# Two chain flows in the written order of a recurrent attention, and z rows kept in the u tile

## The chip, the core and the metric

The kernel runs on one core of one Trainium2 chip. The metric is device time of one execution in microseconds, the median of three runs. The kernel before takes 2223.99 us (2222.03 to 2224.59). A core has TensorE (PE in the profile) for matrix products into PSUM, VectorE (DVE), ScalarE (ACT) and GpSimd (POOL) for elementwise work, and SyncE (SP), whose queue issues all DMAs of this kernel. Each engine works through its own queue in the order in which the program wrote it, and waits at an instruction until what that needs is there.

## The reference

Three parts follow each other. First a recurrent attention: 4 batches x 8 heads, 768 tokens, head dimension 40, with a 40 x 40 state for each head.

```
for t in range(S):
    y[:, :, t] = einsum('bhd,bhde->bhe', r_t, state)
    Sa = einsum('bhde,bhe->bhd', state, a_t)
    state = state * w_t - outer(Sa, b_t) + outer(v_t, k_t)
```

Then a mixture of 8 experts over 3072 tokens of width 320 (hidden width 1024), where every expert computes every token and a gate matrix P, balanced by 8 rounds of row and column scaling, weighs them. Last a network that takes the maximum of three products (width 768) and multiplies it by an output matrix. All is fp32.

## The kernel before

**Blocks and units.** The recurrence over tokens is turned into matrix products over blocks of C = 128 tokens. There are NJ = 6 blocks j and 4 batches b, so 24 units n = 4j + b, each with 8 heads. Batches don't depend on each other; a unit depends on the same batch of the block before through its state. The work of a unit has four parts, written as Python generators:

- `scales` (function `decays`, lines 300 to 339): running products of w on VectorE, `bt` and `at`, and `off` on ScalarE (line 338), a range check. `off` and the result tile `yt` share one buffer.
- `labs` (`lab_grams`): products of `bt` and `at`, copied to `lab` and `ld` by ScalarE. After four units `ld` is turned to `lt`; `invert` inverts its 32 x 32 triangles on GpSimd (block 0 mostly on VectorE), and the result `tt` is turned to `td` on VectorE (line 379).
- `pre`: masked products `lak` (matmul at line 348, mask at line 420), then z (line 475 is its last part). Its first matmuls, tp at line 439, may run once the post of unit n-2 and the chain of unit n-2 are complete (`count["post"] >= n - 1 and count["chain"] >= n - 1`).
- `chain`: a triangular solve in four rows of 32 tokens. For row i: subtract the effect of earlier rows (line 499, i > 0), copy z to `zs` (ScalarE, line 503), multiply by the inverted triangle `td` (line 507), copy the result to `u` (line 511). Each step needs the one before. The chain of unit n may start when pre of unit n is written, post of unit n-2 is complete and `td` of the block exists.
- `post`: turns `u` (ups, line 523), adds up y (lines 534 and 546), updates the state (lines 561 to 569), multiplies and stores y (lines 576 and 579).

**The order.** All parts run in one program order that a planner in the kernel's Python writes while the program is built. Each part yields a `Seg`: an estimated time on TensorE (`pe`), an engine that follows (`eng`, `cost`), what it needs, and a gate on the counts of finished parts. `drive` (line 723) holds one `Flow` for each kind of part and always takes one segment: first a segment without TensorE work that can start now; else the first TensorE segment that can start, in the order of the list of flows (where a running measure of TensorE's load is low, the one with the most load, except that the flow `first`, the chains, goes ahead); else the earliest, with spare matmuls (`idle`, line 708) written into the gap. Beside these flows runs `fill`: parts of the first expert for blocks that are already done, from unit 4 on. The planner's times are its own estimates; they are not measured.

**After the attention.** From about 640 us on `networks` runs the rest of the experts and the last network, with matmuls at lines 215 and 223.

The chains are one flow before the change: `Flow(counted("chain", (chain(n) for n in range(units))))`. `zs` has a single buffer; `u` has two, by n % 2.

Of the kernel before, what the change touches and what calls it, by code (L numbers as in the profile page):

```python
# [9 lines left out]
F32 = mybir.dt.float32  # L10
F32R = mybir.dt.float32r
I32 = mybir.dt.int32
AF = mybir.ActivationFunctionType
# [4 lines left out]
NB, H, S, D = 4, 8, 768, 40  # L18
C = 128
# [14 lines left out]
WARM = 0.55  # L34
# [8 lines left out]
FALL = 0.4  # L43
LATE = 17
SLACK = 0.8
AHEAD = 4
TICK = 10.24 / 3
LAG = 0.2
WLO, WHI = 0.8, 1.25
# [3 lines left out]
def hx(h):  # L53
    return 4 * (h % 2) + h // 2
# [16 lines left out]
def tile_kernel(ctx, tc, em, tm, qr, qk, qv, qw, qa, qb, w_gate, w1, w2, u1, u2, u3, u_out, out):  # L71
    nc = tc.nc

    def pool(stack, name, bufs=1, **kw):
        return stack.enter_context(tc.tile_pool(name=name, bufs=bufs, **kw))
# [170 lines left out]
    ws, xf, first, gate = [{} for _ in pieces], [], [], []  # L246
    order = [NJ - 2, NJ - 1] + list(range(NJ - 2))


    units = NB * NJ  # L250
    with ExitStack() as st:
# [8 lines left out]
        chp = pool(st, "ch")  # L260
# [8 lines left out]
        def jb(n):  # L269
            return n // NB, n % NB  # L270
# [209 lines left out]
        def chain(n):  # L480
            j, b = jb(n)
            d, u = un[n], u_ring[n % 2]
            s = None
            for i in range(4):
                r = slice(32 * i, 32 * i + 32)
                if i == 0:
                    s = Seg(
                        eng="A", cost=0.32, needs=lambda: [d["z_"], blk[j]["t_"]],
                        gate=lambda: count["pre"] > n and count["post"] >= n - 1 and "t" in blk[j],
                    )  # L490
                    yield s
                    zh = d["z"].rearrange("t g a x -> t (g a) x")
                    lab, td = d["lab"], blk[j]["t"]
                    zs = chp.tile([C, H, D], F32, tag="zs", name="zs")
                else:
                    s = Seg(pe=0.23, w=0.3, eng="A", cost=0.32, needs=[s])
                    yield s
                    for h in range(H):
                        nc.tensor.matmul(  # L499
                            zh[r, h, 0:D], lhsT=lab[0:32 * i, hx(h), 32 * i - 32:32 * i], rhs=u[0:32 * i, h, 0:D],  # L500
                            start=False, stop=True, skip_group_check=True, tile_position=(0, 32 * i),
                        )
                nc.scalar.activation(out=zs[r], in_=zh[r, :, 0:D], func=AF.Copy)  # L503
                s = Seg(pe=0.24 if i else 0.62, w=0.25, eng="A", cost=0.32, needs=[s])
                yield s
                for h in range(H):
                    nc.tensor.matmul(  # L507
                        zh[r, h, 0:D], lhsT=td[r, 8 * b + hx(h), :], rhs=zs[r, h, :],
                        start=(h == 0), stop=True, skip_group_check=True, tile_position=(32 * i, 32 * i),
                    )  # L510
                nc.scalar.activation(out=u[r, :, 0:D], in_=zh[r, :, 0:D], func=AF.Copy)
            d["u_"] = s
# [137 lines left out]
        clk = dict(E=2.0, V=2.0, A=3.5, P=6.0, D=1.0, warm=False, acc=0.0, h=0.0)  # L650
        RATE = dict(V=(0.3, 2.1e-3), P=(0.4, 4.5e-3))

        def spend(t, w, floor=False):

            left = t - clk["E"] if floor else t
            while left > 1e-6:
                pace = 1.0 if floor or clk["warm"] else 0.5
                tick = TICK - clk["E"] % TICK
                d = min(left / pace, tick + 1e-6)
                clk["E"] += d  # L660
                clk["acc"] += d * w * (1.0 if clk["warm"] else 0.5) / TICK
                left -= d * pace
                k = 2.0 ** -(d / 1.7)
                clk["h"] = clk["h"] * k + w * (1 - k)
                if d > tick:
                    clk["warm"], clk["acc"] = clk["acc"] >= FALL, 0.0

        count = dict(scale=0, pre=0, chain=0, post=0, lab=0, fill=0, done=0)

        def counted(key, parts):  # L670
            for g in parts:
                yield from g
                count[key] += 1

        def start_of(s):
            t = max(clk["E"], s.after())
            if not s.pe and s.eng:
                t = max(t, clk[s.eng])
            return t

        def take(f):
            s = f.plan
            t = start_of(s)
            if s.pe:
                spend(t, 0.0, True)
                spend(s.pe, s.w)
                t = clk["E"]
            if s.eng:
                t = max(t + LAG if s.pe else s.after(), clk[s.eng]) + s.cost
                clk[s.eng] = t  # L690
            s.done = t + LAG
            f.plan = next(f.gen, None)
# [10 lines left out]
        def idle(n):  # L703

            for _ in range(n):
                if not idler:
                    idler.append(psf.tile([128, 128], F32, tag="f", name="spare"))
                nc.tensor.matmul(idler[0], lhsT=ones, rhs=ones, start=True, stop=True)  # L708
                spend(0.22, 1.0)

        def behind():

            return count["done"] < 2 * (count["post"] - NB) - 1

        def starved(s):

            pace = 1.0 if clk["warm"] else 0.5
            left, want = TICK - clk["E"] % TICK, (HOT - clk["acc"]) * TICK
            d = s.pe / pace
            return 0 < want < left * pace < TICK and want > (d * s.w + max(left - d, 0.0)) * pace and d < left + 1  # L720

        def drive(flows, first):
            while any(f.plan for f in flows):
                order = flows
                if count["lab"] < EARLY:
                    order = flows[0:2] + flows[4:6] + flows[2:4] + flows[6:]
                ready = [f for f in order if f.plan and (f.plan.gate is None or f.plan.gate())]
                now = clk["E"] + 0.02
                side = [
                    f for f in ready  # L730
                    if not f.plan.pe and start_of(f.plan) <= now + (SLACK if f is flows[AHEAD] and count["chain"] else 0.0)
                ]
                if side:
                    take(side[0])
                    continue
                beside = flows[-1] if flows[-1] in ready and start_of(flows[-1].plan) <= now else None
                soon = [f for f in ready if f is not flows[-1] and f.plan.pe and start_of(f.plan) <= now]
                if soon:
                    f = soon[0]
                    if clk["h"] < WARM and f is not first:  # L740
                        f = max(soon, key=lambda f: f.plan.w)
                    if beside and (behind() or starved(f.plan)):
                        take(beside)
                    elif not spare and starved(f.plan):
                        idle(1)
                    else:
                        take(f)
                elif beside:
                    take(beside)
                else:  # L750
                    f = min(ready, key=lambda f: start_of(f.plan))
                    t = start_of(f.plan)
                    n = int((t - clk["E"] - 0.1) / (0.22 if clk["warm"] else 0.44))
                    if n > 0 and not spare and (not DUMMY <= count["post"] < LATE or clk["acc"] < HOT):
                        idle(min(n, 4))
                        continue
                    if not f.plan.pe:
                        spend(t, 0.0, True)
                    take(f)

        with tc.manual_schedule():
            spare, idler = [], []
            mask = k0.tile([C, C], F32, name="mask")
            ends = k0.tile([128, WC], F32, name="ends")
            wmid = k0.tile([HR, 1], F32, name="wmid")
# [20 lines left out]
            for n in range(NB + 1):  # L786
# [13 lines left out]
                out=mask, in_=mask, pattern=[[1, C]], compare_op=ALU.is_gt, fill=0.0, base=0,  # L800
# [50 lines left out]
            def cut(j):  # L851
                return SPLIT if j > 1 else SPLIT1 if j else SPLIT0

            flows = [
                Flow(g for j in range(NJ) if cut(j) < 32 for g in invert(j, nc.vector, "V", cut(j), 32)),
                Flow(g for j in range(NJ) for g in invert(j, nc.gpsimd, "P", 0, cut(j))),
                Flow(counted("chain", (chain(n) for n in range(units)))),
                Flow(counted("pre", (pre(n) for n in range(units)))),
                Flow(scales()),
                Flow(labs()),  # L860
                Flow(counted("post", (post(n) for n in range(units)))),
                Flow(weights()),
                Flow(inputs()),
                Flow(fill()),
            ]
            drive(flows, flows[2])


    def token_by_token():
# [398 lines left out]
```

## Time and profile before

| what | value |
|---|---|
| median of 3 runs | 2223.99 us |
| the profiled execution | 2218.65 us |
| its span, first to last instruction | 2216.9 us |
| TensorE matmul busy | 2161.2 us, 97% |
| VectorE busy | 1081.7 us, 49% |
| ScalarE busy | 609.2 us, 27% |
| GpSimd busy | 283.7 us, 13% |
| mean granted TensorE clock | 0.979 |

A stretch of time with a granted clock of 0.50 is one in which TensorE ran at 1.2 GHz instead of 2.4. "Busy" of TensorE counts spare matmuls too, and a matmul counts from its start to its modelled end, so that neighbours overlap: the time from one start to the next is what it costs in a queue. In the timelines an fp32 matmul is two instructions; a chain group of 8 heads shows as x16.

### The profile page before, as it was taken

The numbers are of one execution on the slowest core, as the hardware profiler recorded it, in microseconds if no ns is written. First come the engines' busy times: TensorE is split into PE (matmuls) and PEld (weight loads), VectorE is DVE, ScalarE is ACT, GpSimd is POOL, SyncE is SP. The second block draws the span as 40 slices with busy tenths as digits, with TensorE's granted clock in tenths as the row PEclk, the third lists the DMA queues.
The fourth block names the chain that finished last, engine by engine and source line by source line (L and its number), as shares of the span: only waits on it lengthen the run. The fifth ranks groups of instructions, "written<-read, shape, count | busy, mean of one in ns | idle before, by whom it ended". The sixth has DMA issues, their size and how long they took to land.

```text
span 2216.9 us, 37608 instructions
## 1 busy us (share of the span) xinstructions
PE 2161.2 (97%) x16083; PEld 1929.9 (87%) x16083; DVE 1081.7 (49%) x1882; ACT 609.2 (27%) x1223; POOL 283.7 (13%) x455
## 2 busy tenths in 40 slices
PE   5989999999999999999999999999999999999999
PEld 5878878788879999999999999999999999988888
DVE  8667665644347456555555333344344343442332
ACT  3444444442232232212222112122122122222221
POOL 5164362541000010011100000000000000000000
PEclk8689999999999999999999999999999999999999
DMA  4143334322142001101101000000000000100000
GB/s 118 49 126 102 94 97 111 83 73 81 54 128 79 24 27 44 59 22 59 42 26 51 18 26 27 1 27 27 1 27 21 7 28 15 54 4 22 12 13 26
DMA packets 70981, 105.41 MB, mean 48 GB/s; under 512 B 7341, under 2 KB 51117, under 8 KB 70805
## 3 DMA queue, kind: packets, MB, share of 16 engines
q1 hardware_dynamic: 70805, 102.92, 16.2%
q8 instruction: 128, 2.10, 0.4%
q14 instruction: 48, 0.39, 0.1%
HBM read 87.81 MB, written 15.07 MB: 46 GB/s over the span
## 4 chain that ended last, share of the span: by engine, by line
PE 89%; ACT 1%; DVE 1%; issue 0%; DMA 0%; SPq 0%; ACTq 0%
PE ps L223 32%; PE ps L215 30%; PE pu L215 9%; PE psg L348 3%; PE z L507 2%; PE fps L215 2%; PE yps L546 2%; PE z L499 2%; PE fps L223 2%; PE z L475 1%; PE dps L561 1%; PE z L459 1%; ACT ld L369 1%; PE yps L534 1%; PE spare L708 1%
## 5 line engine op out<-in xcount | busy, mean ns | idle before, releaser
L223 PE MATMUL ps<-w2h,h 128*128 128x320 f32 x2912 | 655.9, 309 | 0.0
L223 PEld LDWEIGHTS ps<-w2h,h 128*128 128x128 f32 x2912 | 490.6, 188 | 3.6
L226 ACT ACTIVATE h<-ps 128x512 fp32r<-128x512 f32 x364 | 217.8, 598 | 950.1 <-PE ps L215 948.8
L227 DVE SCALAR_TENSOR_TENSOR h<-ps,h 128x512 fp32r<-128x512 f32 x364 | 251.6, 691 | 411.9 <-ACT h L226 410.6
L223 PE MATMUL ps<-w2l,h 128*128 128x320 f32 x1456 | 449.8, 309 | 0.0
L1042 DVE SCALAR_TENSOR_TENSOR acc<-ps,lg,acc 128x320 f32<-128x320 f32 x336 | 184.7, 550 | 255.6 <-PE ps L223 254.2
L215 PE MATMUL ps<-xh,w1l 128*128 128x512 f32 x1092 | 309.3, 391 | 0.0
L215 PE MATMUL ps<-xh,w1h 128*128 128x512 f32 x1092 | 307.6, 390 | 0.0
L223 PEld LDWEIGHTS ps<-w2l,h 128*128 128x128 f32 x1456 | 273.3, 188 | 3.5
L215 PEld LDWEIGHTS ps<-xh,w1h 128*128 128x128 f32 x1092 | 205.4, 188 | 43.6
L215 PEld LDWEIGHTS ps<-xh,w1l 128*128 128x128 f32 x1092 | 201.1, 188 | 35.5
L215 PE MATMUL ps<-xl,w1h 128*128 128x512 f32 x728 | 226.0, 391 | 0.0
L215 PE MATMUL pu<-xh,uq 128*128 128x512 f32 x648 | 169.9, 392 | 0.0
L215 PEld LDWEIGHTS ps<-xl,w1h 128*128 128x128 f32 x728 | 137.0, 188 | 29.3
L215 PEld LDWEIGHTS pu<-xh,uq 128*128 128x128 f32 x648 | 120.3, 188 | 23.9
L420 DVE TENSOR_TENSOR gr<-psg,mask 128x512 f32<-128x512 f32 x144 | 92.6, 685 | 73.8 <-PE psg L348 73.0
L401 POOL TENSOR_TENSOR tmp<-lt,tt 128x87 f32<-128x87 f32 (+24 forms) x186 | 102.1, 549 | 188.1 <-DVE lt L379 174.0
L135 POOL TENSOR_TENSOR f<-f,m 128x384 f32<-128x384 f32 (+2 forms) x24 | 24.4, 1015 | 660.4 <-DVE m L133 402.4
L405 POOL TENSOR_TENSOR tt<-tt,tmp 128x87 f32<-128x87 f32 (+24 forms) x186 | 106.7, 574 | 14.6
L1103 DVE TENSOR_TENSOR g<-pu,g 128x512 f32<-128x512 f32 x72 | 49.8, 692 | 98.3 <-PE pu L215 98.3
L507 PEld LDWEIGHTS z<-zs,td 32*32 32x32 f32 x1536 | 63.3, 110 | 22.2 <-issue 10.0
L507 PE MATMUL z<-zs,td 32*32 32x40 f32 x1536 | 75.2, 202 | 4.2 <-ACT zs L503 4.1
(172 smaller groups left out, 2362.1 us busy)
## 6 DMA issues: line engine op xcount, KB each, us to landing
e<-in_em_dram SPq DMA_DIRECT2D x23, 626.0 KB
r<-in_moe_w_dram SPq DMA_DIRECT2D x32, 320.0 KB
r<-in_moe_w_dram SPq DMA_DIRECT2D x32, 256.0 KB
bk<-in_tm_dram SPq DMA_DIRECT2D x24, 320.0 KB
xr<-ydr SPq DMA_DIRECT2D x10, 512.0 KB
kr<-in_em_dram SPq DMA_DIRECT2D x24, 208.0 KB
vt<-in_em_dram SPq DMA_DIRECT2D x24, 208.0 KB
r<-in_em_dram SPq DMA_DIRECT2D x24, 208.0 KB
```

The costliest lines, as they stand in the source:

```text
L215: nc.tensor.matmul(ps, lhsT=a, rhs=b, start=(n == 0), stop=(n == len(seq) - 1))
L223: nc.tensor.matmul(ps, lhsT=a, rhs=b, start=(n == 0), stop=(n == len(seq) - 1))
L226: nc.scalar.activation(out=h[:, 0], in_=ps, func=AF.Relu)
L227: nc.vector.scalar_tensor_tensor(out=h[:, 1], in0=ps, scalar=0.0, in1=h[:, 0].bitcast(F32), op0=ALU.max, op1=ALU.subtract)
L348: nc.tensor.matmul(ps[a][:, q, :], lhsT=lhs[r, q, :], rhs=rhs[r, q, :], start=(q == 0), stop=True, skip_group_check=True, tile_position=(6 ...
L401: eng.tensor_tensor(out=t, in0=lt[:, m:m + 1, m + 1:32].to_broadcast([128, n, w]), in1=tt[:, 0:n, m:m + 1].to_broadcast([128, n, w]), op=A ...
L405: eng.tensor_tensor(out=tt[:, 0:n, m + 1:32], in0=tt[:, 0:n, m + 1:32], in1=t, op=ALU.subtract)
L420: nc.vector.tensor_tensor(out=t, in0=ps, in1=mask.unsqueeze(1).to_broadcast([C, HP, C]), op=ALU.mult)
L499: nc.tensor.matmul(zh[r, h, 0:D], lhsT=lab[0:32 * i, hx(h), 32 * i - 32:32 * i], rhs=u[0:32 * i, h, 0:D], start=False, stop=True, skip_gro ...
L507: nc.tensor.matmul(zh[r, h, 0:D], lhsT=td[r, 8 * b + hx(h), :], rhs=zs[r, h, :], start=(h == 0), stop=True, skip_group_check=True, tile_po ...
L1042: nc.vector.scalar_tensor_tensor(out=acc[:, i], in0=ps, scalar=pr[:, i, e:e + 1], in1=acc[:, i], op0=ALU.mult, op1=ALU.add,)
L1103: nc.vector.tensor_tensor(out=g, in0=ps, in1=g, op=ALU.max)
```

## The change

There are two flows of chains, one for the even and one for the odd units. Each goes through its units in order; `count["chain"]` now counts the units whose chains are complete without a gap (`solved`). Both flows stand where the one stood, ahead of `pre`, and both are "first". The chain of unit n+1 no longer has to follow the end of the chain of unit n; its gate is the same. Since two chains may now be open at a time, the single buffer `zs` is given up: z of a row is copied into the rows of `u` where the result will stand, and `td` multiplies it from there. The position of `scales` in the list and the slices of the list move by one.

```
-AHEAD = 4
+AHEAD = 5
...
-                    zs = chp.tile([C, H, D], F32, tag="zs", name="zs")
...
-                nc.scalar.activation(out=zs[r], in_=zh[r, :, 0:D], func=AF.Copy)
+                nc.scalar.activation(out=u[r, :, 0:D], in_=zh[r, :, 0:D], func=AF.Copy)
...
-                        zh[r, h, 0:D], lhsT=td[r, 8 * b + hx(h), :], rhs=zs[r, h, :],
+                        zh[r, h, 0:D], lhsT=td[r, 8 * b + hx(h), :], rhs=u[r, h, 0:D],
...
+        def linked(ns):
+
+            for n in ns:
+                yield from chain(n)
+                solved.add(n)
+                while count["chain"] in solved:
+                    count["chain"] += 1
...
-                    order = flows[0:2] + flows[4:6] + flows[2:4] + flows[6:]
+                    order = flows[0:2] + flows[5:7] + flows[2:5] + flows[7:]
...
-                    if clk["h"] < WARM and f is not first:
+                    if clk["h"] < WARM and f not in first:
...
-            spare, idler = [], []
+            spare, idler, solved = [], [], set()
...
-                Flow(counted("chain", (chain(n) for n in range(units)))),
+                Flow(linked(range(0, units, 2))),
+                Flow(linked(range(1, units, 2))),
...
-            drive(flows, flows[2])
+            drive(flows, flows[2:4])
```

## Rows read from the trace of the kernel before

**Rows 1.** Stages of the span: us, busy us of each engine (instructions), TensorE clock, DMA.
```profile
60.00:94.40 34.40, 34.40 (x261) 31.16 (x259) 17.32 (x25) 15.62 (x44) 2.48 (x2) 0.50 0.22 61
...
110.00:180.00 70.00, 60.78 (x821) 52.14 (x820) 46.68 (x75) 29.33 (x73) 37.62 (x55) 0.88 0.44 118
180.00:590.00 410.00, 400.62 (x5420) 345.55 (x5417) 229.75 (x370) 165.09 (x398) 154.96 (x254) 0.99 0.33 90
...
645.00:2216.90 1571.90, 1566.53 (x8630) 1415.24 (x8628) 709.21 (x1262) 357.18 (x605) 49.33 (x48) 1.00 0.10 31
```

**Rows 2.** The same view for spare matmuls alone (PE, PEld, clock, DMA).
```profile
83.27:93.17 9.90, 4.50 (x16) 3.61 (x16) 0.50 0.01 2
93.17:105.90 12.73, 2.09 (x14) 1.71 (x14) 0.93 0.06 18
110.00:180.00 70.00, 6.00 (x32) 4.38 (x32) 0.88 0.44 118
```

**Rows 3.** Timeline of TensorE around units 0 and 1: start, us, instruction.
```profile
79.83 3.63 PE L475 MATMUL z<-v,gr 128*128 128x40 f32 x16
...
83.97 1.27 PE L507 MATMUL z<-zs,td 32*32 32x40 f32 x16
...
87.10 2.93 PE L708 MATMUL spare<-ones 128*128 128x128 f32 x12
89.96 1.27 PE L507 MATMUL z<-zs,td 32*32 32x40 f32 x16
91.16 2.08 PE L348 MATMUL psg<-at,bt 64*128 64x128 f32 x16
93.17 1.10 PE L523 MATMUL ups<-ident,u 128*104 128x128 f32 x4
...
105.33 0.64 PE L546 MATMUL yps<-gr,kb 128*40 128x128 f32 x8
...
109.47 0.64 PE L523 MATMUL ups<-ident,u 128*104 128x128 f32 x4
```

**Rows 4.** Timeline of ScalarE: first copy of chain 1, and off of unit 8.
```profile
96.76 0.41 ACT L503 ACTIVATE zs<-z 32x320 f32<-32x320 f32 x1
...
109.88 0.72 ACT L338 ACTIVATE off<-e,wmid 104x512 f32<-104x512 f32 x1 [0.47 <-DMA ydr<-yt]
```

**Rows 5.** Timeline of TensorE: last groups of chains 1 and 22, first group of chain 4.
```profile
108.19 0.76 PE L507 MATMUL z<-zs,td 32*32 32x40 f32 x16
...
111.14 1.98 PE L475 MATMUL z<-v,gr 128*128 128x40 f32 x16
...
171.12 0.76 PE L507 MATMUL z<-zs,td 32*32 32x40 f32 x16
...
587.00 0.76 PE L507 MATMUL z<-zs,td 32*32 32x40 f32 x16
587.68 1.98 PE L475 MATMUL z<-v,gr 128*128 128x40 f32 x16
```

**Rows 6.** Timeline of SP's queue: store of y, load of e for unit 9.
```profile
106.73 1.54 SPq L579 DMA_DIRECT2D ydr<-yt  x2
...
111.96 0.33 SPq L274 DMA_DIRECT2D e<-in_em_dram  x1
```

**Rows 7.** Timeline of VectorE: scales of unit 9, mask of post 1, td of block 1.
```profile
119.60 0.54 DVE L315 TENSOR_SCALAR e<-e 128x512 f32<-128x512 f32 x1 [5.01 <-DMA e<-in_em_dram]
...
124.70 1.29 DVE L420 TENSOR_TENSOR gr<-psg,mask 128x512 f32<-128x512 f32 x2
...
167.80 2.05 DVE L379 STREAM_TRANSPOSE td<-tt 128x1024 f32<-128x1024 f32 x1
```

**Rows 8.** Timeline of GpSimd: its first instruction after the inversion of block 1.
```profile
169.90 0.95 POOL L390 MEMSET tt<- 128x1024 f32 x1 [20.43 <-DVE td L379]
```

**Rows 9.** Groups by line on ScalarE: busy us, mean ns | idle before.
```profile
L511 ACT ACTIVATE u<-z 32x320 f32<-32x320 f32 x96 | 41.1, 428 | 107.7 <-PE z L507 106.4
L503 ACT ACTIVATE zs<-z 32x320 f32<-32x320 f32 x96 | 40.8, 425 | 92.9 <-PE z L499 84.0 <-PE z L475 8.2
```

## The prediction

> **What bounds the kernel now.** I read the stages first, then the spare matmuls in them, then the order of single instructions around the chains. The stage table [rows 1] shows a TensorE that is never free: from 645 us to the end it works 1566.53 of 1571.90 us at the full clock, on networks that the change doesn't touch; from 180 to 590 us, units 4 to 22 of the attention beside the early part of the networks, it works 400.62 of 410. So only the order of the attention can move the end, and only where TensorE holds time that isn't work. There are two such stretches before 180 us. From 60 to 94.4 us TensorE is busy without a break, but at the half clock, 0.50; from 110 to 180 us it is idle for 70.00 - 60.78 = 9.2 us. Some of the busy time is padding: spare matmuls take 4.50 us between 83.27 and 93.17, 2.09 us between 93.17 and 105.90, 6.00 us between 110 and 180 [rows 2].
>
> **Where the order can change.** A chain is eight ScalarE copies with seven groups of 16 matmul instructions (L507 four times, L499 three times) between them. Chain n+1 may start when z of unit n+1 has been issued. Before the change it must also wait for the end of chain n, and that is all that the second flow takes away. So I looked, for each n, which comes first: the last L507 group of chain n or the last L475 group of unit n+1. Of 23 pairs 22 have L507 first; the first and the last of these stand in [rows 5], 108.19 before 111.14 and 587.00 before 587.68. In them chain n is already issued when its neighbour becomes possible, and the new freedom is empty. One pair is the other way round: z of unit 1 ends at 83.27 (start 79.83, next instruction 83.27), while chain 0 goes on until the instruction at 91.16 [rows 3], and chain 1's first copy runs only at 96.76 [rows 4]. The reason is the gate of unit n+1's work ahead of its chain: it wants the post of unit n-1 done, which runs beside chain n and lasts about as long. Unit 1 has no such post to wait for.
>
> **What that one overlap is worth.** Chain 1 can start some 13 us sooner (83.7 against 96.76). What counts is what it displaces.
> Step 1, 83.27 to 93.17, half clock: chain 0 has three groups left, 1.20 us each from start to start (89.96 to 91.16). Then come 2.01 us of products (91.16 to 93.17), so of 9.90 us 4.29 are left, the spare runs: 0.70 before 83.97, 2.86 from 87.10 to 89.96, and 0.73 as the rest [rows 2, 3]. Nothing of chain 1 is ready for the first. A group of chain 1 in the second costs 1.20 - 0.73 = 0.47 more; one in the third saves 2.86 - 1.20 = 1.66. So ups of unit 0, the start of post 0 at 93.17 [rows 3], comes 1.2 us sooner, with two of chain 1's seven later groups out of the way.
> Step 2, 93.17 to 105.90, post 0: today five groups of chain 1 lie in it, 0.68 us each at the full clock (as 587.00 to 587.68, [rows 5]), and two behind it. Afterwards the remaining five lie in it, so the work is the same; only spares can go, from nothing to 2.09 us [rows 2]. The groups of post 0 also wait for VectorE's masks, which nothing shortens, so I take the middle, 1.0. Post 0, whose last group starts at 105.33 [rows 3], ends 2.2 us sooner than 105.90.
> Step 3, post 1 and chain 2: two chain groups (1.36 us, the second at 108.19) and the 0.60 us of spares behind that one vanish ahead of ups of unit 1 at 109.47 [rows 3]; it can come 2.2 + 2.0 = 4.2 us sooner. But the end of post 1 doesn't hang on it. The store of y goes to SP's queue at 106.73, and the load of e for unit 9 stands behind it at 111.96 [rows 6]; off of unit 8 on ScalarE waited for that store, 109.88 [rows 4]. VectorE then stands 5.01 us for e at 119.60, and the mask that post 1 needs is behind it at 124.70 [rows 7]. That train starts with the end of post 0, and moves by 2.2. Between 2.2 and 4.2 I take 3.0, nearer to the lower end because of the train.
> Step 4, the rest: what is 3.0 us early at 130 us stays so, since from 180 us TensorE is the bound and its work is the same; the early part of the networks is held by x of block 0, which moves along.
>
> **The other edits.** Copying z to u instead of zs: L503 into zs costs 425 ns, L511 into u 428 [rows 9], so 96 x 3 ns = 0.3 us on ScalarE, which is idle most of each stage (165.09 of 410 us busy from 180 us on, [rows 1]): nothing; without that cover it would be the 0.3. The copy waits, as before, for the matmuls whose result it reads, and the earlier readers of u are in a post that the gate wants finished. No wait is new behind which another queue would stand, and no DMA is added; POOL and SP keep their instructions. The constant 5 and the reordered list name the same flows as before. Bounds of all this: -0.3 to +0.5 us, zero taken.
>
> **Sum.** The profiled execution took 2218.65 us, 1.75 more than its span of 2216.9, and is 5.3 us under the median of 2223.99. 2218.65 - 3.0 = 2215.65; on the median's scale 2223.99 - 3.0 = 2221.0. About 0.2%, 4.4 us, is what a measurement of this kernel can tell from no change, so the likeliest case lies inside.
>
> **Rivals.**
> A second window: masks before e. If post 1 runs 4.2 us earlier while e's planned time moves by 2.2, the planned order on VectorE can put post 1's mask ahead of unit 9's scales. Then the 5.01 us wait and some 4 of the 5.10 us between 119.60 and 124.70 leave post 1's path: -9 in all, 2215. For it: mask and scales stand next to each other in [rows 7]. Against: the margin must be eaten by 2 us, and VectorE would still have to stand for e ahead of the masks of the next unit.
> Overlaps everywhere: if the earlier units let z of unit n+1 pass chain n in block 0 too, half of the idle 9.2 and the spare 6.00 us of 110 to 180 go, on top of 3.0, and some of the clock's loss there (0.88): -13, 2211. Against: the 22 pairs.
> Nothing arrives: td of block 1 is turned on VectorE at 167.80 [rows 7], chain 4 uses it at 171.12 [rows 5], though GpSimd had been idle 20.43 us at 169.90 [rows 8]: the written order, with its own idea of the inversion's end, places it. Units 1 to 3 may come early only to stand there: 2224. Against: GpSimd is truly done by then, so a real wait needn't appear, and unit 5 may now overlap chain 4.
> Slower, the clock: from 60 to 94.4 us it is 0.50, from 180 us on 0.99 or 1.00 [rows 1]. Ahead of the rise TensorE ran the spares from 87.10 and the products at 91.16 [rows 3]; the change puts 32x32 groups in the place of those spares. If the rise came only with the end of post 0, some 11 us later, a group would cost 1.20 instead of 0.68, so 11 us at the half level hold 6.2 us of work at the full: 4.8 lost. If one further stretch of that length between 110 and 180 falls to the half level, some 4 more: 3.0 gained, 9 lost, 2230. It decides from 7 us of added half clock on (7 x 0.43 = 3.0).
> The Trainium skill, TensorE: Matmul & The Clock Gate, section "Part 1: The HAM clock gate", speaks for this rival: the throttled level (1.2 GHz) is the default, and activity releases it. The trace agrees on the two levels [rows 1].
> Side by side: two groups on different 32x32 corners of the array could run at once, which would make up to three groups of chain 1 free at 1.20 us: -3.6 more, 2217.4. Against: the 16 instructions of a group all sit on one corner, and only neighbours in the queue could pair. The products at 91.16, which change halves with every instruction, take 2.01 us for 16, 126 ns each, and the transposes of 128 columns at 93.17 take 1.03 us for 4, 257 each [rows 3]: pairing shows where it alternates by instruction.
> This is what the Trainium skill says in TensorEngine Tiling (Array Packing), "Key Properties": tiles operate independently. By it alone the sum would be 2217.4.
>
> **Chances.** Forecast 0.40 (its own range 2217 to 2224; 0.14 of it beyond the 0.2%), masks before e 0.14, overlaps everywhere 0.09, side by side 0.03, nothing arrives 0.14, slower clock 0.20 (0.05 of it too small to tell). Faster 0.14 + 0.14 + 0.09 + 0.03 = 0.40; slower 0.15; within, 0.45. For the range I go down to 2211, the overlaps, and up to 2230, the clock: what is left out is half of the overlaps and a worse clock, under 0.2.
>
> **What would show it.** Right: chain 1's first copy (now an activation into u) before 86 us; fewer spares from 83 to 93 us; ups of unit 0 near 92, of unit 1 near 105; the two orders otherwise alike, with the same events some 3 us earlier from 130 us to 610 us; the stage from 645 us as long as before. Wrong: half clock well beyond 95 us; masks before the scales of unit 9 on VectorE; more than one or two pairs with L475 before the last L507; spare matmuls or idle time near 160 to 170 us that take up the lead; or an order from 180 us on that differs so much that cold stretches there outweigh the start.

## The result and the profile after

The changed kernel takes 2236.25 us (median of 9 runs, 2231.96 to 2241.85), the kernel before 2223.99 (9 runs beside them, 2210.19 to 2226.67). The ratio is 1.007, interval 1.0055 to 1.0084: slower by 12 to 19 us, and 12.3 between the medians. That lies above the forecast range of 2211 to 2230 us: 0.5% to 0.8% slower, where a small gain was the likeliest case.

The stages of the changed kernel (us, busy us of TensorE, its weight loads, VectorE, ScalarE, GpSimd with instructions, then TensorE's clock, DMA share and GB/s) answer to [rows 1]:

```profile
60.00:94.40 34.40, 33.43 (x355) 30.13 (x353) 20.73 (x29) 20.35 (x56) 3.39 (x6) 0.67 0.25 67
...
110.00:180.00 70.00, 66.04 (x725) 57.02 (x724) 37.80 (x63) 23.80 (x59) 25.13 (x39) 0.65 0.35 94
180.00:590.00 410.00, 400.50 (x5318) 345.55 (x5317) 231.02 (x371) 162.14 (x392) 154.69 (x254) 0.96 0.33 90
...
645.00:2230.50 1585.50, 1577.99 (x8679) 1423.97 (x8678) 713.94 (x1270) 361.51 (x612) 49.26 (x48) 1.00 0.10 31
```

What to see: from 110 to 180 us TensorE is busier than before (66.04 against 60.78 us) and does less (725 instructions against 821), because its clock is 0.65 there instead of 0.88. Idle time has turned into half-speed time. From 645 us on little differs but the start. The spare matmuls alone, to set beside [rows 2]:

```profile
83.27:93.17 9.90, 2.81 (x12) 2.29 (x12) 0.70 0.01 2
93.17:105.90 12.73, 2.02 (x14) 1.49 (x12) 1.00 0.26 62
110.00:180.00 70.00, 7.96 (x30) 6.10 (x30) 0.65 0.35 94
```

The overlap is there, and only there where it was foreseen. The timeline of TensorE around units 0 and 1 (start, us, instruction) answers to [rows 3]:

```profile
77.97 1.98 PE L475 MATMUL z<-v,gr 128*128 128x40 f32 x16
...
81.00 1.21 PE L506 MATMUL z<-u,td 32*32 32x40 f32 x32 [0.74 <-ACT u L502]
...
84.16 1.07 PE L498 MATMUL z<-u,lab 32*32 32x40 f32 x13
...
85.18 1.06 PE L506 MATMUL z<-u,td 32*32 32x40 f32 x13
86.17 2.08 PE L348 MATMUL psg<-at,bt 64*128 64x128 f32 x16
88.18 1.68 PE L715 MATMUL spare<-ones 128*128 128x128 f32 x8
89.79 0.76 PE L506 MATMUL z<-u,td 32*32 32x40 f32 x16
90.48 0.65 PE L522 MATMUL ups<-ident,u 128*104 128x128 f32 x4
...
101.66 0.57 PE L439 MATMUL tp<-ident,ip 104*128 104x104 f32 x4
...
105.55 0.64 PE L522 MATMUL ups<-ident,u 128*104 128x128 f32 x4
```

At 81.00 two groups of 16 run in one go, the third of chain 0's L506 groups and the first of chain 1. The first matmuls of `pre`, tp, serve as milestones below: those of unit 2 stand at 101.66 instead of 105.90, of unit 4 at 152.34 instead of 155.69 (start of the stage that follows), of unit 6 at 204.36 instead of 197.34. So the change is 3.35 us ahead at unit 4 and 7.0 behind at unit 6; it ends 13.6 us behind. Even the lead is in part work put off. At its tp of unit 4 the changed kernel still has two groups of chain 3 and one run of lab's products to do:

```profile
152.84 0.76 PE L498 MATMUL z<-u,lab 96*32 96x40 f32 x16
...
154.63 0.76 PE L506 MATMUL z<-u,td 32*32 32x40 f32 x16
...
156.74 1.16 PE L348 MATMUL psg<-at,bt 64*128 64x128 f32 x16
```

In the old order the same three stand ahead of that tp (in the first experiment below at 150.29, 152.51 and 153.71, with tp at 156.73).

The loss between unit 4 and unit 6 has one face. The stage from tp of unit 4 to tp of unit 6 takes 52.02 us in the changed kernel:

```profile
152.34:204.36 52.02, 48.15 (x583) 40.86 (x581) 32.71 (x51) 19.90 (x49) 8.29 (x14) 0.77 0.32 90
```

and 40.85 in a kernel with the order of the kernel before (the first experiment; the second line is the kernel before itself):

```profile
156.73:197.58 40.85, 38.04 (x537) 32.96 (x535) 31.80 (x50) 17.99 (x43) 3.92 (x5) 0.95 0.36 105
155.69:197.34 41.65, 38.45 (x536) 33.02 (x535) 32.82 (x50) 18.42 (x45) 3.83 (x5) 0.96 0.40 112
```

At a clock of 0.77, 2 x 0.23 x 52.02 = 23.9 us of the stage ran at 1.2 GHz, against 2 x 0.05 x 40.85 = 4.1. By the group times of the prediction (0.43 lost per us at the half level) that is 8.5 us. The 46 instructions more are the work put off, 48, less one spare matmul (two instructions): from start to start 0.69 + 0.68 + 1.09 us, about 2.2 with the spare taken off. Together 10.7 of the 11.2 us. The stage comes out alike in other profiles: 40.84 and 41.65 us at 0.95 and 0.96 in experiments 4 and 8, which have the old order, 51.91 to 55.58 us at 0.74 to 0.79 in experiments 2, 3 and 9, which have the new one (the longest, experiment 2, holds 14 added spare matmuls). Against experiment 1 the changed kernel is 4.4 us ahead at unit 4, 6.8 behind at unit 6 and 8.4 behind at the end, so most of that loss falls into this stage.

### The profile page after: what moved, and what is told of

It is laid out like the page before. It is cut to its first block, busy times and chain, and to the rows that moved or that the text cites. A ratio compares the mean times of both kernels' runs of the same rounds, so it can differ in the third digit from the quotient of the medians.

```text
span 2230.5 us, 37666 instructions
## 1 busy us (share of the span) xinstructions
PE 2175.7 (98%) x16071; PEld 1942.5 (87%) x16071; DVE 1081.5 (48%) x1882; ACT 609.3 (27%) x1223; POOL 281.9 (13%) x455
## 4 chain that ended last, share of the span: by engine, by line
PE 93%; DVE 3%; ACT 2%; issue 1%; DMA 1%; SPq 0%; POOL 0%; ACTq 0%; DVEq 0%
PE ps L223 32%; PE ps L215 30%; PE pu L215 9%; PE psg L348 4%; PE z L506 3%; PE yps L545 2%; PE z L498 2%; PE fps L215 2%; PE z L475 2%; PE fps L223 2%; ACT ld L369 1%; PE dps L560 1%; PE spare L715 1%; PE z L459 1%; PE yps L533 1%
## 5 line engine op out<-in xcount | busy, mean ns | idle before, releaser
L215 PEld LDWEIGHTS pu<-xh,uq 128*128 128x128 f32 x648 | 120.2, 188 | 23.9
L506 PEld LDWEIGHTS z<-u,td 32*32 32x32 f32 x1536 | 66.0, 114 | 23.5 <-issue 10.6
L506 PE MATMUL z<-u,td 32*32 32x40 f32 x1536 | 77.9, 206 | 5.5 <-ACT u L502 5.4
```

The source lines that it names most:

```text
L215: nc.tensor.matmul(ps, lhsT=a, rhs=b, start=(n == 0), stop=(n == len(seq) - 1))
L506: nc.tensor.matmul(zh[r, h, 0:D], lhsT=td[r, 8 * b + hx(h), :], rhs=u[r, h, 0:D], start=(h == 0), stop=True, skip_group_check=True, tile_p ...
```

## The experiments

A table first, since one reading runs through all of them. Each execution lists its span and its mean granted clock; span x 2 x (1 - clock) is its time at the half clock. Means over all executions (those of the kernel before from the four comparisons of the experiments; their four means lie between 2217.7 and 2219.9 us, so a us or two in the table says little). The factor 0.4 is chosen so that the first eight rows agree:

| kernel | runs | mean us | half clock, us | mean - 0.4 x half |
|---|---|---|---|---|
| before | 98 | 2219.0 | 95 | 2181 |
| no overlap | 12 | 2220.7 | 97 | 2182 |
| before, 8 spares fewer | 12 | 2218.0 | 95 | 2180 |
| before, td early | 12 | 2224.3 | 109 | 2181 |
| chain 4 between | 12 | 2224.4 | 111 | 2180 |
| chain 4 late | 12 | 2226.6 | 112 | 2182 |
| the change, true groups | 12 | 2230.0 | 122 | 2181 |
| the change | 9 | 2236.0 | 138 | 2181 |
| spares in chain 2 | 6 | 2237.5 | 131 | 2185 |
| spares in chains 2 and 4 | 6 | 2239.1 | 130 | 2187 |
| before, gap filled | 12 | 2217.9 | 73 | 2188 |
| the change, gap filled | 6 | 2232.6 | 116 | 2186 |
| between, gap filled | 12 | 2220.5 | 90 | 2185 |
| before, true groups | 12 | 2226.5 | 100 | 2187 |

**1. No overlap.** The gate of the chain gets one more condition:

```
+ gate=... and (n != 1 or count["chain"] >= 1),
```

> The change with one condition added: the chain of unit 1 also waits until the chain of unit 0 is complete. Everything else of the change stays, z in the u tile and two flows. The written order of every engine is then instruction for instruction the order of the kernel before. Theory A (the cost comes from the order that follows the one overlap of chains 0 and 1): 2224 us, ratio to before 0.998 to 1.002. Theory B (z in the u tile, or the two flows as such, cost the time): near the changed kernel, 2232 to 2240, ratio 1.005 or more.

Measured: 2221.9 us, ratio 1.0002 (0.9986 to 1.0019). Theory A: with chain 1 held back the order is the old one, and so is the time. The u tile, the new counts and the second flow cost nothing. The ScalarE rows of the changed kernel say the same, 426 and 428 ns beside the 425 and 428 of [rows 9]:

```profile
L510 ACT ACTIVATE u<-z 32x320 f32<-32x320 f32 x96 | 41.1, 428 | 112.8 <-PE z L506 111.2
L502 ACT ACTIVATE u<-z 32x320 f32<-32x320 f32 x96 | 40.9, 426 | 93.8 <-PE z L498 84.3 <-PE z L475 8.8
```

This run's profile also stands nearer to that of the changed kernel than the profile of before does: in both the clock rose at 75.7 us and fell at 82.5, while before had it at the half level until 94.8. Its timeline of TensorE:

```profile
78.03 1.98 PE L475 MATMUL z<-v,gr 128*128 128x40 f32 x16
...
83.48 2.78 PE L715 MATMUL spare<-ones 128*128 128x128 f32 x12
86.19 0.76 PE L506 MATMUL z<-u,td 32*32 32x40 f32 x16
86.87 1.16 PE L348 MATMUL psg<-at,bt 64*128 64x128 f32 x16
87.97 0.65 PE L522 MATMUL ups<-ident,u 128*104 128x128 f32 x4
...
100.70 0.58 PE L439 MATMUL tp<-ident,ip 104*128 104x104 f32 x4
...
104.32 0.65 PE L522 MATMUL ups<-ident,u 128*104 128x128 f32 x4
```

Without the overlap ups of unit 0 comes 2.5 us sooner (87.97 against 90.48), tp of unit 2 1.0 sooner, ups of unit 1 1.2 sooner. But the clock is not quite the same: without the overlap it is back at the full level at 86.0 us, in the changed kernel only at 89.3. The stretch between, first the changed kernel, then experiment 1 (engines as in the stages above):

```profile
86.00:89.30 3.30, 3.30 (x25) 2.99 (x24) 0.00 (x0) 2.86 (x8) 0.00 (x0) 0.50 0.00 0
```

```profile
86.00:89.30 3.30, 3.03 (x40) 2.36 (x39) 0.00 (x0) 1.62 (x6) 0.00 (x0) 1.00 0.00 0
```

At 0.43 lost per us these 3.3 us are worth 1.4, an estimate. So at ups of unit 0 about 1 us of the 2.5 is the order's, and at tp of unit 2 the order alone would be up to half a us ahead: close to nothing. The lead of 4.2 us that the changed kernel seemed to have over the profile of before at 101.66 was the clock's. The longer dip is not of this pair alone. Of the profiles in these two orders whose clock rose at 73 to 76 us, the two without the overlap (experiments 1 and 8) have it fall again for 3.4 us, the five with it (the change, experiments 2, 5, 9 and 10) for 6.8 to 20.5 us.

**2 and 3. Spares in chains 2 and 4, and in chain 2 alone.** Behind each group:

```
+ extra(2 if n in (2, 4) else 0)     # two matmuls like idle(), without spend(); chain 2 alone: n in (2,)
```

> The changed kernel with two spare matmuls behind each of the seven groups of chain 2 and of chain 4, 28 in all, which the planner doesn't know of, so that the rest of its order stays. They lie at 112 to 131 us and 162 to 185 us, in the two long stretches at the half clock (109.8 to 143.9 and 164.4 to 188.3 us in the profile of the changed kernel). They cost up to 28 x 0.32 = 9 us at the full clock. Theory 1 (the cost of the change is the half clock between 108 and 190 us): these stretches shrink from 58 us to 25 or less, the time falls by 5 to 15 us, to 2221 to 2231. Theory 2 (the new order itself puts waits on the path, the clock only goes along): the clock may rise, but the time stays or grows by up to 9, 2236 to 2245.

> As the run with spares in chains 2 and 4, but in chain 2 alone: 14 spare matmuls, up to 4.5 us. It tells which of the two cold stretches carries the cost. Theory 1, both cost alike per us: the first stretch of 34 us shrinks, the second of 24 stays, and the time lies half way, 2227 to 2234. If the first is hidden (unit 4 still came 3.35 us early behind it in the profile of the changed kernel) and only the second costs: no gain, 2235 to 2241. Theory 2: 2236 to 2241.

Measured: 2238.28 us (1.0083, 1.0052 to 1.0115) and 2238.18 (1.0079, 1.0057 to 1.0101). Both miss the fall that theory 1 forecast and lie in the ranges of theory 2. The half clock falls only by 7 to 9 us of 138 on the mean; by the table's last column the spares cost some 6 us for 28 and 4 for 14. Padding put into the stretch bought less than it cost. That neither refutes theory 1 nor shows theory 2, for the clock hardly moved.

**4. The kernel before with eight spares fewer.**

```
+ if count["post"] != 1:
      nc.tensor.matmul(idler[0], lhsT=ones, rhs=ones, start=True, stop=True)
```

> The kernel before, with its order, without the eight spare matmuls that it holds between 108.88 and 122 us (their planned time is kept, the instructions are left out). Theory 1 (TensorE's level there hangs on that padding): the clock falls there some 15 us sooner than in the kernel before and comes back late, +5 to +12 us, 2229 to 2236. Theory 2 (padding is only padding): 8 x 0.32 = 2.6 us less at most, 2221 to 2224.

Measured: 2218.16 us, 0.9987 (0.9972 to 1.0001). That is under both ranges, which count from 2223.99; by the ratio nothing changed. The spares that the old order had beside chain 2 are not what kept it fast: theory 1 in that form is out. The mean half clock is 95 us with them and without.

**5 to 7. Where chain 4 lies.** In the changed kernel lab of unit 7, which waits for chain 0, is followed at once by the turn of lt; the inversion of block 1 starts 12 us earlier, and the planner turns td at 156.31 instead of 167.80 [rows 7]. VectorE of the changed kernel (scales of unit 9 first, no longer waiting for e; then the mask of post 1):

```profile
109.32 0.88 DVE L315 TENSOR_SCALAR e<-e 128x512 f32<-128x512 f32 x1
...
118.80 1.29 DVE L420 TENSOR_TENSOR gr<-psg,mask 128x512 f32<-128x512 f32 x2 [1.48 <-PE psg L348]
...
156.31 2.08 DVE L379 STREAM_TRANSPOSE td<-tt 128x1024 f32<-128x1024 f32 x1
```

So chain 4 starts 8.5 us sooner than at 171.12 [rows 5] and lies between the pieces of post 3, TensorE of the changed kernel:

```profile
162.60 0.76 PE L506 MATMUL z<-u,td 32*32 32x40 f32 x16 [1.25 <-ACT u L502]
...
166.62 1.67 PE L545 MATMUL yps<-gr,kb 128*40 128x128 f32 x8 [2.63 <-DVE gr L420]
168.22 1.27 PE L498 MATMUL z<-u,lab 32*32 32x40 f32 x16
...
172.32 1.27 PE L506 MATMUL z<-u,td 32*32 32x40 f32 x16
173.52 2.08 PE L348 MATMUL psg<-r,ut 64*128 64x128 f32 x16
...
182.32 0.96 PE L439 MATMUL tp<-ident,ip 104*128 104x104 f32 x4
```

With the old order (experiment 1) it starts behind the last products of post 3 and runs beside the next unit's `pre`:

```profile
170.43 1.56 PE L348 MATMUL psg<-r,ut 64*128 64x128 f32 x16
171.92 0.76 PE L506 MATMUL z<-u,td 32*32 32x40 f32 x16
...
175.78 0.57 PE L439 MATMUL tp<-ident,ip 104*128 104x104 f32 x4
176.29 0.76 PE L498 MATMUL z<-u,lab 64*32 64x40 f32 x16
```

A group is 0.69 us there (171.92 to 172.61, where a spare begins) and 1.20 in the changed kernel (172.32 to 173.52). Three kernels move chain 4. Up to tp of unit 4 their order on TensorE is that of the kernel they are made from, but for one or two spare matmuls:

```
5: + gate=... and (n != 4 or "ru" in un[3]),   # set behind post 3's gram(ut, rt)
6: kernel before, invert(): cost=(...) * (0.6 if j == 1 else 1)
7: changed kernel, invert(): cost=(...) * (1.12 if j == 1 else 1)
```

> The changed kernel with one condition added: the chain of unit 4 waits until post 3 has issued its last products (line 348, u by r), as it happens to do in the kernel before. The overlap of chains 0 and 1 stays. Theory P (the cost sits in one place: block 1's td is turned earlier, so chain 4 runs between the pieces of post 3 instead of beside the next unit's work, and TensorE stays at the half clock there): the stage from tp of unit 4 to tp of unit 6, 52 us in the changed kernel and 41 before, is 41 to 45 again, the half clock in it under 12 us, the time 2217 to 2226. Theory Q (the early cold stretch from 110 to 144 us, or the changed order from 190 us on, costs the time): 2230 to 2240.

> The kernel before, one flow, with one planning number changed: the planned time of block 1's inversion is multiplied by 0.6. No instruction is added or left out but a spare or two; td of block 1 is turned earlier in VectorE's order, and chain 4 then lies between the pieces of post 3 in the same sequence as in the changed kernel. Theory P: slow like the changed kernel, 2230 to 2238, with some 20 us more of half clock between 160 and 200 us and 50 us or more from tp of unit 4 to tp of unit 6. Theory Q: 2217 to 2226.

> The changed kernel with the planned time of block 1's inversion multiplied by 1.12: chain 4's first group comes after the first sums of post 3 (line 545) but before its last products, so between the changed kernel and the one with chain 4 held back. Theory P, a matter of degree: stage from tp of unit 4 to tp of unit 6 between 42 and 52 us, 2222 to 2232. Theory Q: 2230 to 2240.

Measured: chain 4 late 2227.37 us, 1.0037 (1.0020 to 1.0054); before with td early 2224.98, 1.0023 (1.0004 to 1.0041); chain 4 between 2222.81, 1.0019 (0.9999 to 1.0038). The stage from tp of unit 4 to tp of unit 6, first chain 4 late, then before with td early, then chain 4 between:

```profile
154.51:205.16 50.65, 44.67 (x578) 38.51 (x576) 32.02 (x50) 19.80 (x48) 9.14 (x16) 0.84 0.32 92
```

```profile
152.58:200.80 48.22, 46.61 (x534) 39.52 (x533) 30.19 (x49) 18.61 (x45) 6.05 (x12) 0.75 0.33 95
```

```profile
154.50:214.21 59.71, 58.33 (x579) 50.34 (x577) 32.73 (x50) 19.79 (x48) 9.28 (x16) 0.61 0.28 78
```

Theory P is half right. The old kernel with chain 4 moved forward does get slower and its stage goes cold (0.75, 48.22 us), with the same instructions; the changed kernel with chain 4 moved back or half back gets faster. But each recovers or costs a third to three quarters of the change's 0.7%: the time of experiment 6 lies in theory Q's range, that of experiment 5 between the two, and the stage did not come back to 41 to 45 us where P wanted it. The last profile is a warning: it is the slowest of that kernel's 12 executions (2234.97 us), and its stage of 59.71 us is at 0.61, while the fastest (2216.35) had the same instructions. On the mean the three have 109 to 112 us of half clock, between 95 and 138. So the place of chain 4 moves 14 to 27 of the 44 us of added half clock. In the written order of TensorE little else is left to make the others. Spare matmuls left out, the changed kernel and these three have from tp of unit 8 to the end the 13561 instructions of the kernel before in the same sequence, and from unit 6 to unit 8 all but one. So the others must come from the order ahead of unit 6, which the overlap changes from 81 us on; experiments 5 and 7 have that order up to unit 4, and experiment 6 has the old one.

**8 to 10. The idle gap filled.** In three kernels the wait from 37.3 to 55.4 us is filled:

```
+ extra(72 if n == NB else 0)        # ahead of unit 4's products
  for a, ps in enumerate(products(bt, at)):
```

> The kernel before with 72 spare matmuls added in the stretch from 37.3 to 55.4 us, in which its TensorE is idle (18.12 us, waiting for at of unit 4). 33 spares in a row took 7.53 us, so 72 take 16.4 us and end before the wait does; nothing else changes. Over the nine profiled executions so far the time follows the time at the half clock between 40 and 700 us: 2218.65 us at 85.3 (before), 2223.8 at 95.8 (same order), 2232.2 at 129.6 (the change), 0.32 us per us, whatever the order. Theory K (the half clock is the cause of the time): the stretch at the half clock that starts at 40 us ends sooner or starts later, by 15 to 40 us, and the time falls by 0.32 us for each, 5 to 13 us, to 2207 to 2216. Theory L (the half clock only goes along with waits that are there anyway): the clock changes, the time stays, 2217 to 2223.

> The changed kernel with the same 72 spare matmuls in the same idle stretch ahead of unit 4's products; its order is the same as that of the kernel before up to 79 us. Theory K: as there, 5 to 13 us less than the changed kernel, 2222 to 2230, and still over the kernel before with the spares by about what the later cold stretches cost. Theory L: 2231 to 2238.

> The changed kernel with chain 4 between (planned time of block 1's inversion multiplied by 1.12), with the same 72 spare matmuls. If theory K holds and the overlap of chains 0 and 1 is worth anything at the full clock, this is the fastest of the three, 2205 to 2214; if the overlap is worth nothing, it equals the kernel before with spares within 3 us; theory L: 2219 to 2225.

Measured: before 2216.98 us, 0.9996 (0.9981 to 1.0011); the change 2233.89, 1.0059 (1.0043 to 1.0074); between 2217.72, 1.0005 (0.9985 to 1.0025). Theory K's forecast fails in the first two, whose times are those of theory L. The third is within 3 us of the first, as theory K has it for an overlap that is worth nothing, and 5 us under the same kernel without the 72 spares (2222.81); theory L gave 2219 to 2225. The half clock falls by about 22 us in each, but some 15 of these lay in the gap itself, where TensorE had no work to slow down; the clock fell again at 55.4 to 56.3 us, as soon as the gap was over. Half clock in the gap had cost next to nothing. None of the three beats the kernel before.

**11 and 12. The planner told how long a group takes.**

```
- s = Seg(pe=0.23, w=0.3, eng="A", ...)
+ s = Seg(pe=0.66, w=0.11, eng="A", ...)
...
- s = Seg(pe=0.24 if i else 0.62, w=0.25, eng="A", ...)
+ s = Seg(pe=0.66, w=0.11, eng="A", ...)
```

> The kernel before with another planning estimate: a chain group counts 0.66 us of TensorE (0.68 from start to start in the trace at the full clock) with a load of 0.11, instead of 0.23 to 0.24 us with 0.25 to 0.3. The planner then writes another order and other spares; no other work changes. Over all runs the mean time follows the mean time at the half clock (75 runs of the kernel before: 96 us and 2219.5; 9 of the changed kernel: 138 us and 2236.0). Theory M (the order decides how long TensorE is at the half clock, and the planner misplaces it because its estimate of a group is a third of the real one): half clock under 85 us on the mean, 2207 to 2215. Theory N (the planner's estimate doesn't matter, any new order lands anywhere): 2215 to 2235, with time and half clock again on the same line.

> The changed kernel with the same estimate of a chain group. Theory M: as the kernel before with it, within 4 us. Theory N: anywhere from 2215 to 2240 on the line of time against half clock, 2181 + 0.4 x half clock in us.

Measured: 2227.35 us, 1.0043 (1.0023 to 1.0064), and 2228.34, 1.0055 (1.0033 to 1.0077). Theory M fails: a truer estimate of this one term gives an order that is slower than the old one, though the two kernels do lie within 4 us of each other. The changed kernel with it lies on the line again (122 us, 2230.0); the kernel before with it lies 5 us above the line, so there the order itself has some cost beside the clock.

## Why the prediction was wrong

**Where the order changes: right.** One pair overlaps, chains 0 and 1, and with that one overlap taken away the order and the time are those of before (experiment 1). The other edits cost nothing, as forecast.

**Step 1, ups of unit 0 sooner by 1.2 us: wrong.** It came 2.5 us later with the overlap than without (90.48 against 87.97), some 1.4 by the clock and about 1 by the order. I counted the spare runs as free places for chain 1. In the new order the products of lab and a spare run of four (86.17 to 89.79) and one more group of chain 1 still stand ahead of ups.

**Step 2 and 3: no gain up to unit 3.** Post 0 ends at 101.66 instead of 100.70 without the overlap; with the clock's 1.4 us taken off, the order gained at most half a us there, not 2.2. The wait for e did go: the load is now issued ahead of the store of y, on SP's queue of the changed kernel

```profile
102.17 0.31 SPq L274 DMA_DIRECT2D e<-in_em_dram  x1
102.73 1.02 SPq L578 DMA_DIRECT2D ydr<-yt  x2
```

where [rows 6] had the store 5.2 us ahead of the load. So the train on which I hung step 3 dissolved, and by unit 3 it had brought nothing, because TensorE fell to the half clock at 109.8 us and became what post 1 waited for: tp of unit 3 is at 124.84, with the old order at 124.87.

**Step 4, "what is 3.0 us early at 130 us stays so": the step that failed.** It took TensorE's work as the bound from 180 us on and its pace as given. The work is indeed the same; the pace is not. In the profiles 3.35 us of lead at unit 4 became 7.0 us of lag at unit 6; against experiment 1 the stage is 11.2 us longer, of which 8.5 are half clock (23.9 us of it against 4.1) and 2.2 the work put off. That the lead at unit 4 came out near the forecast 3.0 us was in part luck. From 55.40 us to tp of unit 4, first before, then the changed kernel:

```profile
55.40:155.69 100.29, 93.37 (x1074) 81.52 (x1074) 60.70 (x96) 44.13 (x118) 45.45 (x71) 0.74 0.29 76
55.40:152.34 96.94, 93.72 (x1019) 82.36 (x1019) 59.69 (x96) 42.83 (x114) 43.98 (x71) 0.68 0.30 79
```

TensorE stood idle for 3.2 us instead of 6.9, which is a gain of the order. It had some 3.5 us less to do, 2.5 of them the work put off and the rest spares; and by its lower clock it lost about as much again.

**The rival "slower, the clock" named the mechanism and was short in size.** It put the added half clock up to the end of post 0 and one stretch behind it, 22 us, and gave 2230 us with a chance of 0.20. The first place is borne out by the longer dips under experiment 1; the largest stretch, from unit 4 to unit 6, it did not name. The means show 44 us more, 95 to 138. At the 0.31 us per us found among the kernel before's own executions that is 13.5 us, at the 0.43 of the group times 18.8; the means lie 17 us apart, 14.5 against the nine executions beside the change. The rule that I set beside it, the Trainium skill's in TensorE: Matmul & The Clock Gate, "Part 1: The HAM clock gate", says that activity releases the throttled level. In the stage from unit 4 to unit 6 TensorE was busy for 93% of the time in either order (48.15 of 52.02 us, 38.04 of 40.85), at clocks of 0.77 and 0.95; what sets the two apart no run shows. "Nothing arrives" named the place, not the effect: td of block 1 is placed by the planner's own idea of the inversion's end, and its earlier place took chain 4 with it, where I had expected work to stand and wait. I had judged that GpSimd's true end made this harmless.

**How far the cause is shown.** The line of the table is strong evidence: eight kernels with seven different orders lie within 2 us of 2181 + 0.4 x half clock (the other six lie 4 to 8 us above it, five of them with added spares), and the 98 executions of the kernel before, one program, spread from 2207.01 to 2228.14 us along the same trend (0.31 us per us, correlation 0.96). No run sets the clock by itself with everything else fixed; the one attempt that moved it much (8 to 10) moved it mainly where TensorE was idle. That the overlap is what starts it is shown by experiment 1, and that chain 4's place is a part of it from both sides (experiments 5 to 7). Chain 4 moved in the old order costs 0.23%, the overlap with chain 4 moved back 0.19 to 0.37%, both together 0.70%; with intervals of some 0.2% either way the two can make up all of it. How the remaining 17 to 30 us of half clock divide between the order up to unit 4 and the two coming together stays open, and so does why these orders hold TensorE longer at 1.2 GHz.

## What to carry to other kernels

Before counting an overlap as a gain, ask at what pace the engine will run behind it: here the same instructions took longer because more of them ran at 1.2 GHz, and most of that not where the overlap was. A written order is one piece; follow an edit through the planner's due times to the next place where it decides (here td of block 1, 75 us later). And where executions of one program differ by 1%, set their granted clock against their time before explaining a difference of 0.7% between two programs.

## What the runs showed of the hardware

One program's time at the half clock is not fixed: profiles of the same order (the kernel before and experiment 1) have it rise at 94.8 and at 75.7 us, with the same instructions up to there, and the 98 executions of the kernel before have mean clocks from which 62 to 125 us follow. Two chain groups on different corners of the array do run side by side, a little: the groups at 84.16 (L498) and 85.18 (L506) of the changed kernel alternate by single instructions between 84.97 and 85.18 and take 2.01 us together at the half clock, where 2 x 1.20 = 2.40 were expected; those at 81.00 took 1.33 together, where 2 x 0.68 = 1.36 were. The rule of TensorEngine Tiling (Array Packing), "Key Properties", in the Trainium skill, that tiles operate independently, holds here for 0.4 us and not for the 3.6 that it was given as a bound.
